# Smaller weight loads, all q, k and v loads on one queue, and a new order of the normalisation in an attention and SwiGLU kernel

## The chip, the cores and the metric

The kernel runs on one core of a Trainium2 chip. The metric is the time of one execution in device microseconds (us); three runs give a median of 669.23 us (668.39 to 670.3). TensorE multiplies matrices (PE in the profile, PEld its weight loads), VectorE is DVE, ScalarE is ACT; SP is the queue that issues most transfers, and ACT can issue transfers too.

## The reference

Sigmoid attention for 4 batches, 12 heads, 448 positions and 64 dimensions, whose output goes token by token (1792 tokens of 768 values) through an RMS norm and a SwiGLU block with 1536 hidden values:

```python
def _attn_ref(q, k, v) -> np.ndarray:
    S = q.shape[2]
    scale = 1.0 / np.sqrt(q.shape[-1])
    scores = scale * np.matmul(q, k.transpose(0, 1, 3, 2)) - np.log(S)
    attn = 1.0 / (1.0 + np.exp(-scores))
    return np.matmul(attn, v).astype(np.float32)

def _moe_ref(x, w_gate, w_val, w_out, rms_g) -> np.ndarray:
    rms = np.sqrt(np.mean(x * x, axis=-1, keepdims=True) + 1e-06)
    xn = x / rms * rms_g
    g = xn @ w_gate
    silu = g * (1.0 / (1.0 + np.exp(-g)))
    val = xn @ w_val
    return (silu * val @ w_out).astype(np.float32)
```

q, k and v are float32; the three weight matrices are float64 in memory.

## The kernel before

The order of the work is written out by hand; every engine runs its instructions in the order in which the program emits them.

**Attention.** The 24 pairs of heads (4 batches of 6 pairs) are worked off one after the other, each in four groups g = 0 to 3 (two instructions of scores after two of them, then the products with v of the two groups before: one round of the loop over n; a pair is two rounds). For a pair i, `load_qk` loads q and k (224 KB each), DVE splits them into two float16 parts (`qk_hi`, `qk_lo`), a DMA transpose on SP turns them (`transpose`, tile xc), DVE swaps two halves of the turned k (`k_swap`), and TensorE makes the scores (`scores`, tile sc). ACT applies the sigmoid, TensorE multiplies by v (`av`). The table `FILL` says what is emitted behind the scores of which group, for a pair one to three ahead. `v_mid` copies the seventh block of 128 rows of v, which the two heads share, to a tile of its own by DVE. At the end of a pair ACT squares the result, and DVE adds the squares up (L235). Four buffers hold q and k (`ld_b`), three hold v.

**Work in the background.** The list `later` holds parts with a cost each; `run_later` emits some of them behind every group, on a credit of 0.52 a call. It holds the split of the first two blocks of weights (`split_w`: from float64 words to float32, seven combinations, two float16 parts each) and, at the end of each batch, `norm`: `squares` (TensorE, tile ssq), `mean`, `guess` and three `newton` (DVE, tiny), `spread`, `rows` (TensorE, tile rinv), and then `scale`, sums, `hi` (ACT) and `lo` (DVE) over 128 x 1344 elements. Odd batches make five slots of the input and have eleven such large DVE instructions, even ones four.

**SwiGLU.** Twelve blocks of weights by two halves of the tokens make 24 calls of `quad`, which gets four products out of seven (tiles ca, cb, cd, cc, each product nine matmuls), with DVE and ACT forming the sums. The first two calls run with the norm of the last batch as filling (`fill` emits five parts of `later` at each of five places); the later ones with the split of the next block. `load_w` loads one block of w_gate and one of w_val (768 KB each). At the end TensorE multiplies by w_out (tile o).

**Completions.** Every transfer takes one of eight completion semaphores in turn, whichever queue issues it, and its issue waits until the transfer that held that semaphore before has landed.

The lines of the profile are those of the listing:

Of the kernel before, what the change touches and what calls it, by code (L numbers as in the profile page):

```python
# [24 lines left out]
def attention_then_swiglu(  # L25
# [43 lines left out]
    WARM = 20  # L69
    W_FROM = 4  # L70
    SHARE = 0.52
# [93 lines left out]

    def load_qk(i, queue=nc.scalar):
        t = ld_b[i % 4]
        queue.dma_start(t[:, 0], rows_of(q, i, "(p c) d -> p c d"))
        queue.dma_start(t[:, 1], rows_of(k, i, "(c p) d -> p c d"))

    def load_v(i):
        nc.sync.dma_start(v_b[i % 3], rows_of(v, i, "(c p) d -> p c d"))


# [14 lines left out]
    def k_swap(i):  # L189
        T = t_b[i % 3]  # L190
        nc.vector.tensor_copy(T[D:, 2], T[:D, 1])
        nc.vector.tensor_copy(T[:D, 2], T[D:, 1])  # L192

    def v_mid(i):

        for j in range(2):
            rows = slice(64 * j, 64 * j + 64)
            nc.vector.tensor_copy(v3[i % 3][rows, j], v_b[i % 3][rows, MID])

# [19 lines left out]
    def av(i, g):  # L219
        b, hp = pairs[i]  # L220
        a = at.pop((i, g))
        if g == 0:
            pav[i] = bank("av")
        ps = pav[i]
        for j in range(2):
            w = v3[i % 3][:, j] if g == MID else v_b[i % 3][:, g + j * NG]
            nc.tensor.matmul(  # L227
                ps[64 * j : 64 * j + 64, :S], w, a[:, 0 if g == MID else j], start=(g == 0), stop=(g == MID)
            )
        if g == MID:  # L230
            sq = sq_b[i % 2] if hp else acc_b[b % 2]
            nc.scalar.activation(sq, ps[:, :S], AF.Square)
            nc.scalar.activation(x_b[b % 3][:, hp], ps[:, :S], AF.Copy, scale=g_sb[:, hp : hp + 1])
            if hp:
                tt(acc_b[b % 2], acc_b[b % 2], sq, ALU.add)  # L235
            del pav[i]
# [3 lines left out]
    def norm(b):  # L240
# [51 lines left out]

        parts = [(squares, 0.2), (wait, 0.7), (mean, 0.2), (guess, 0.5)] + [(newton, 0.5)] * 3
        parts += [(spread, 1.1), (rows, 0.2), (wait, 0.7)]
        if not odd:
            for s in range(2):
                parts += [(lambda s=s: scale(s), 1.6)] + hi(s, x[:, s])
                parts += [(wait, 0.7), (lambda s=s: lo(s, x[:, s]), 1.6)]
            return parts
        x0 = x_b[(b - 1) % 3].rearrange("p (k c) s -> p k c s", k=2)  # L300
        s1, s2, s4 = s_b
        queue = [(s1, x[:, 0], x[:, 1], ALU.add, 3), (s2, s1, x0[:, 0], ALU.subtract, 4)]
        queue += [(s4, x0[:, 1], s2, ALU.subtract, 6), (x[:, 0], x0[:, 0], x[:, 0], ALU.subtract, 5)]
        parts += [(lambda: scale(1), 1.6)] + hi(2, x[:, 1]) + [(lambda: scale(0), 1.6)]
        behind = (2, x[:, 1])
        for o, f0, f1, op, slot in queue:
            parts += [(lambda o=o, f0=f0, f1=f1, op=op: tt(o, f0, f1, op), 1.6)]  # L307
            parts += hi(slot, o)
            parts += [(lambda a=behind: lo(*a), 1.6)]
            behind = (slot, o)  # L310
        return parts + [(wait, 0.7), (lambda a=behind: lo(*a), 1.6)]

# [16 lines left out]

    def load_w(fc):  # L330
        for kind in range(2):
            nc.sync.dma_start(
                raw_w[kind].rearrange("p c f w -> p c (f w)"),
                (w_gate, w_val)[kind][:, 2 * fc * P : 2 * fc * P + 2 * P].rearrange("(c p) f -> p c f", p=P),
            )

    def split_w(fc):


        t = win[fc % 2].rearrange("p l s c f -> p l s (c f)")  # L340
        first, second = [], []
        for kind in range(2):
            f = wf[:, 2 * kind : 2 * kind + 2].rearrange("p s f -> p (s f)")
            *parts, last = to_f32(f, raw_w[kind].rearrange("p c f w -> p (c f) w"))
            first += [(x, 0.9) for x in parts]

            def end(last=last, kind=kind):
                last()
                if kind and fc + 1 < NFC:
                    load_w(fc + 1)  # L350

            first.append((end, 1.0))
# [122 lines left out]
    def run_later(share):  # L475
        credit[0] = min(credit[0] + share, 1.6)
        while later and credit[0] > 0:
            part, cost = later.pop(0)
            part()
            credit[0] -= cost  # L480

    def ahead_by(n, part):
        return lambda i: part(i + n) if i + n < len(pairs) else None

    FILL = (
        (ahead_by(2, qk_hi), ahead_by(3, load_qk)),
        (ahead_by(2, qk_lo), ahead_by(1, k_swap)),
        (ahead_by(0, v_mid),),
        (ahead_by(2, transpose), ahead_by(2, load_v)),
# [8 lines left out]
    with tc.manual_schedule():  # L498

        ps = bank("warm")  # L500
        for _ in range(WARM):
            nc.tensor.matmul(ps[:, :P], ones, ones, start=True, stop=True)
        for i in range(3):
            load_qk(i, nc.sync)
        for i in range(2):
# [8 lines left out]
        for n in range(0, len(todo) + 2, 2):  # L514
# [5 lines left out]
            for i, g in todo[max(n - 2, 0) : n]:  # L520
                av(i, g)
                b, hp = pairs[i]
                if hp == NPAIR - 1 and g == MID:
                    later.extend(norm(b))
                run_later(SHARE)
            if n == W_FROM:
                load_w(0)
            if n == W_FROM + 8:
                for fc in range(2):
# [5 lines left out]
        for fc, n in order:  # L535
# [26 lines left out]

            def fill(at, parts=parts):
                if parts is later:
                    for _ in range(5):
# [66 lines left out]
```

## Time and profile before

| | |
|---|---|
| median of three runs | 669.23 us |
| the profiled execution: its time, its span | 667.66 us, 665.9 us |
| PE busy | 624.7 us (94%) |
| DVE, ACT busy | 415.8 us (62%), 244.7 us (37%) |
| mean granted clock of TensorE | 0.979 |
| SP's queue, ACT's queue | 48.97 MB, 12.39 MB |

Busy times and shares are of the span, from the first to the last instruction of the core; the time has 1.8 us more around it. A share over the whole says little here, since the program has stages with different limits: the attention and the first two quads lie in the first 230 us, the rest of the quads up to 492 us, and the product with w_out behind that.

### The profile page before, as it was taken

How to read it: one execution, taken by the hardware profiler on the slowest of the kernel's cores; microseconds unless marked ns; L12 is line 12 of the kernel's file. 1: busy time of each engine (PE TensorE's matmuls, PEld its weight loads, DVE VectorE, ACT ScalarE, POOL GpSimd, SP SyncE). 2: the span in 40 equal slices, each digit the busy share in tenths (PEclk: the TensorE clock that was granted, in tenths of full speed). 3: DMA queues.
4: the chain of work that ended last, by engine and by line, in shares of the span. 5: the costliest groups of instructions: out<-in, count | busy, mean ns of one | idle time of the engine just before them, and what ended most of it. 6: DMA issues, size and time to landing. Idle time of an engine off the chain costs nothing.

```text
span 665.9 us, 8450 instructions
## 1 busy us (share of the span) xinstructions
PE 624.7 (94%) x3368; PEld 314.6 (47%) x3368; DVE 415.8 (62%) x675; ACT 244.7 (37%) x372; POOL 0.7 (0%) x6
## 2 busy tenths in 40 slices
PE   7895798998989799999999999999999989999997
PEld 5331233332334355555555555555546646666664
DVE  4395798797737889888888888988777710000000
ACT  2574656786754432432333233243232220000000
POOL 0000000000000000000000000000000000000000
PEclk8997999998999899999999999999999989999999
DMA  9999976787700032033023112112344031101111
GB/s 186 246 235 140 242 162 139 145 175 157 115 4 1 1 94 67 29 95 95 1 94 96 35 62 94 59 38 94 118 187 169 1 96 36 35 26 36 36 36 35
DMA packets 116855, 61.89 MB, mean 93 GB/s; under 512 B 90192, under 2 KB 115280, under 8 KB 116816
## 3 DMA queue, kind: packets, MB, share of 16 engines
q1 hardware_dynamic: 92400, 48.97, 29.7%
q10 hardware_dynamic: 24416, 12.39, 7.8%
q8 instruction: 26, 0.43, 0.3%
q14 instruction: 13, 0.11, 0.1%
HBM read 44.83 MB, written 5.51 MB: 76 GB/s over the span
## 4 chain that ended last, share of the span: by engine, by line
PE 77%; DVE 10%; DMA 6%; issue 3%; ACT 3%; ACTq 1%; SPq 0%; DVEq 0%
PE o L454 24%; PE cd L384 11%; PE cc L384 11%; PE ca L384 11%; PE av L227 6%; PE sc L213 6%; PE cb L384 6%; DMA xc<-xc 5%; DVE xc L291 2%; DVE room L307 1%; DVE room L235 1%; ACT room L215 1%; DVE room L282 1%; DVE xc L192 1%; DMA xc<-in_k_dram 1%
## 5 line engine op out<-in xcount | busy, mean ns | idle before, releaser
L384 PEld LDWEIGHTS <-wr 128*128 128x128 f16 x1512 | 148.4, 98 | 144.5 <-issue 7.8
L454 PE MATMUL o<-xc,room 128*128 128x384 f16 x798 | 134.8, 329 | 3.7 <-ACT room L465 2.2
L454 PEld LDWEIGHTS <-room 128*128 128x128 f16 x798 | 78.6, 99 | 56.8 <-issue 4.1
L215 ACT ACTIVATE room<-sc,bias_s 128x896 f32<-128x896 f32 x96 | 84.2, 915 | 56.9 <-PE sc L213 51.6
L213 PE MATMUL sc<-xc 128*128 128x448 f16 (+1 forms) x384 | 80.6, 372 | 18.8 <-DMA xc<-xc 13.0
L384 PE MATMUL cd<-xc,wr 128*128 128x448 f16 x432 | 90.2, 354 | 3.0 <-DVE room L408 2.6
L384 PE MATMUL cc<-xc,wr 128*128 128x448 f16 x432 | 90.7, 356 | 1.6 <-DVE room L424 1.6
L227 PE MATMUL av<-room 128*64 128x448 f32 x384 | 84.7, 564 | 0.0
L213 PEld LDWEIGHTS <-xc 128*128 128x128 f16 (+1 forms) x384 | 29.6, 103 | 81.9 <-issue 47.5
L465 ACT ACTIVATE room<-o 128x384 f32<-128x384 f32 x28 | 13.7, 490 | 113.1 <-PE o L454 109.3
L415 ACT ACTIVATE room<-ca 128x448 f32<-128x448 f32 x24 | 13.0, 542 | 94.4 <-PE ca L384 94.4
L384 PE MATMUL cb<-xc,wr 128*128 128x448 f16 x216 | 44.8, 352 | 0.0
L384 PE MATMUL ca<-room,wr 128*128 128x448 f16 x216 | 44.8, 352 | 0.0
L384 PE MATMUL ca<-xc,wr 128*128 128x448 f16 x216 | 44.8, 352 | 0.0
L227 PEld LDWEIGHTS av<-room 128*64 128x64 f32 x384 | 26.5, 141 | 35.9 <-issue 31.4
L360 DVE SCALAR_TENSOR_TENSOR wr<-wr 128x768 f16<-128x768 f32 (+1 forms) x48 | 39.0, 850 | 0.1
L357 ACT ACTIVATE wr<-wr 128x768 f16<-128x768 f32 (+1 forms) x48 | 34.1, 751 | 0.0
L419 ACT ACTIVATE room<-room 128x448 f32<-128x448 f32 x24 | 13.9, 577 | 51.5 <-DVE room L418 51.5
L326 DVE SCALAR_TENSOR_TENSOR wr<-wr 128x768 uint32<-128x768 uint32 x31 | 29.7, 958 | 1.0
L327 DVE SCALAR_TENSOR_TENSOR wr<-wr 128x768 uint32<-128x768 uint32 x31 | 29.6, 955 | 0.7
L399 ACT ACTIVATE room<-ca 128x448 f32<-128x448 f32 x24 | 13.0, 543 | 39.8 <-PE ca L384 39.3
L181 DVE SCALAR_TENSOR_TENSOR xc<-xc 128x896 f16<-128x896 f32 x24 | 26.1, 1090 | 0.6
(65 smaller groups left out, 483.3 us busy)
## 6 DMA issues: line engine op xcount, KB each, us to landing
wr<-in_moe_w_gate_dram SPq DMA_DIRECT2D x12, 768.0 KB, 4.5
wr<-in_moe_w_val_dram SPq DMA_DIRECT2D x12, 768.0 KB, 4.4
room<-in_v_dram SPq DMA_DIRECT2D x24, 224.0 KB, 4.1
wr<-in_moe_w_out_dram SPq DMA_DIRECT2D x7, 768.0 KB, 4.3
xc<-in_q_dram ACTq DMA_DIRECT2D x21, 224.0 KB, 3.4
xc<-in_k_dram ACTq DMA_DIRECT2D x21, 224.0 KB, 4.6
xc<-in_moe_w_out_dram SPq DMA_DIRECT2D x4, 768.0 KB, 8.6
out_dram<-room SPq DMA_DIRECT2D x28, 96.0 KB, 2.1
```

The source lines that it names most:

```text
L181: stt(n[:, :, :, 1], ld_b[i % 4], SQ, n[:, :, :, 0], ALU.mult, ALU.subtract)
L213: nc.tensor.matmul(o, m, r, start=(w == 0), stop=(w == 1))
L215: nc.scalar.activation(a[:, :n], ps[:, :n, :S], AF.Sigmoid, bias=bias_s, scale=1.0 / (math.sqrt(D) * SQ * SQ))
L227: nc.tensor.matmul(ps[64 * j : 64 * j + 64, :S], w, a[:, 0 if g == MID else j], start=(g == 0), stop=(g == MID))
L326: lambda: stt(b, r[:, :, 0], 29, b, ALU.logical_shift_right, ALU.bitwise_or),
L327: lambda: stt(b, r[:, :, 1], 0xC0000000, b, ALU.bitwise_and, ALU.bitwise_or),
L357: nc.scalar.activation(t[:, 0, s], wf[:, s], AF.Copy, scale=SW)
L360: stt(t[:, 1, s], wf[:, s], SW, t[:, 0, s], ALU.mult, ALU.subtract)
L384: nc.tensor.matmul(ps, w[:, l, b, c], xc[n, a][:, r, c], start=(not more and c == 0 and m == 0), stop=(c == NK - 1 and m == 2), skip_group ...
L419: nc.scalar.activation(y[:, 1], y[:, 1], AF.Silu, scale=UNIT)
L454: nc.tensor.matmul(ps[:, :HALF], h[c, t // NTOK][:, l, t % NTOK * P : t % NTOK * P + P], wo[c][:, r, e * HALF : e * HALF + HALF], start=(c ...
L465: nc.scalar.activation(o, ps[:, :HALF], AF.Copy, scale=1.0 / (SH * SO))
```

## The change

- `load_qk` always issues from SP, and for the pair four ahead instead of three; four pairs are loaded at the start.
- `v_mid` is gone; `load_v` fills that tile by two more transfers of 64 x 64 values.
- `load_w` puts its work on a list `loads`, in parts of two of six blocks of rows (256 KB, three per matrix). `run_load` issues one part at the end of each round of the attention, and two at each `fill` of a quad. The first load starts at n = 2 instead of n = 4, the first split at n = 14 instead of n = 12. The next block's load of a matrix is put on the list when that matrix's words have been read, no longer when both have.
- The sum of squares is a part of `later` (cost 0.6, put at its front) instead of an instruction emitted at once.
- `wait` costs nothing but ends the call of `run_later`; there are three ahead of `squares`, two behind it, three ahead of `rows` and two behind it.
- The parts of an odd norm are in the order of the slots' use: 4, 5, 3, 2, 6 instead of 2, 3, 4, 6, 5.

```diff
-    W_FROM = 4
+    W_FROM = 2
...
-    def load_qk(i, queue=nc.scalar):
+    def load_qk(i):
         t = ld_b[i % 4]
-        queue.dma_start(t[:, 0], rows_of(q, i, "(p c) d -> p c d"))
-        queue.dma_start(t[:, 1], rows_of(k, i, "(c p) d -> p c d"))
+        nc.sync.dma_start(t[:, 0], rows_of(q, i, "(p c) d -> p c d"))
+        nc.sync.dma_start(t[:, 1], rows_of(k, i, "(c p) d -> p c d"))
 
     def load_v(i):
         nc.sync.dma_start(v_b[i % 3], rows_of(v, i, "(c p) d -> p c d"))
+
+        b, hp = pairs[i]
+        for j in range(2):
+            n = (MID * P + 64 * j) % S
+            nc.sync.dma_start(v3[i % 3][64 * j : 64 * j + 64, j], v[b, 2 * hp + j, n : n + 64])
...
-    def v_mid(i):
-
-        for j in range(2):
-            rows = slice(64 * j, 64 * j + 64)
-            nc.vector.tensor_copy(v3[i % 3][rows, j], v_b[i % 3][rows, MID])
...
             if hp:
-                tt(acc_b[b % 2], acc_b[b % 2], sq, ALU.add)
+                later.insert(0, (lambda: tt(acc_b[b % 2], acc_b[b % 2], sq, ALU.add), 0.6))
...
-        parts = [(squares, 0.2), (wait, 0.7), (mean, 0.2), (guess, 0.5)] + [(newton, 0.5)] * 3
-        parts += [(spread, 1.1), (rows, 0.2), (wait, 0.7)]
+        parts = [(wait, 0.0)] * 3 + [(squares, 0.2)] + [(wait, 0.0)] * 2 + [(mean, 0.2), (guess, 0.5)] + [(newton, 0.5)] * 3
+        parts += [(spread, 1.1)] + [(wait, 0.0)] * 3 + [(rows, 0.2)] + [(wait, 0.0)] * 2
...
+        parts += [(lambda: scale(0), 1.6), (lambda: scale(1), 1.6)]
+        parts += [(lambda: tt(s1, x[:, 0], x[:, 1], ALU.add), 1.6)] + sub(s2, s1, x0[:, 0])
+        parts += both(4, s2, sub(s3, x0[:, 0], s3)) + both(5, s3, sub(s4, x0[:, 1], s2))
+        return parts + both(3, s1) + both(2, x[:, 1]) + both(6, s4)
...
+    loads = []
+
+    def load_w(fc, kind):
+
+
+        def part(c):
+            src = (w_gate, w_val)[kind][c * P : (c + 2) * P, 2 * fc * P : 2 * fc * P + 2 * P]
+            dst = raw_w[kind][:, c : c + 2].rearrange("p c f w -> p c (f w)")
+            nc.sync.dma_start(dst, src.rearrange("(c p) f -> p c f", p=P))
+
+        loads.extend((fc, lambda c=c: part(c)) for c in range(0, NCC, 2))
+
+    def run_load():
+        if loads:
+            loads.pop(0)[1]()
...
             credit[0] -= cost
+            if part is wait:
+                break
...
-        (ahead_by(2, qk_hi), ahead_by(3, load_qk)),
+        (ahead_by(2, qk_hi), ahead_by(4, load_qk)),
         (ahead_by(2, qk_lo), ahead_by(1, k_swap)),
-        (ahead_by(0, v_mid),),
+        (),
...
+            run_load()
             if n == W_FROM:
-                load_w(0)
-            if n == W_FROM + 8:
+                load_w(0, 0)
+                load_w(0, 1)
+            if n == W_FROM + 12:
```

On SP's queue, from the transpose of the third pair on (xc<-xc is a transpose, room<-in_v_dram is v, wr a part of the weights), before:

```order
L184 DMA_TRANSPOSE xc<-xc 128x14x128
L172 DMA room<-in_v_dram 128x7x64
L332 DMA wr<-in_moe_w_gate_dram 128x6x256
L332 DMA wr<-in_moe_w_val_dram 128x6x256
L184 DMA_TRANSPOSE xc<-xc 128x14x128
L172 DMA room<-in_v_dram 128x7x64
L184 DMA_TRANSPOSE xc<-xc 128x14x128
L172 DMA room<-in_v_dram 128x7x64
```

And the same queue now, one pair later, where the parts of the weights run:

```order
L189 DMA_TRANSPOSE xc<-xc 128x14x128
L172 DMA room<-in_v_dram 128x7x64
L177 DMA room<-in_v_dram 64x64 x2
L340 DMA wr<-in_moe_w_gate_dram 128x2x256
L168 DMA xc<-in_q_dram 128x448
L169 DMA xc<-in_k_dram 128x7x64
L340 DMA wr<-in_moe_w_gate_dram 128x2x256
L189 DMA_TRANSPOSE xc<-xc 128x14x128
```

Between two transposes there now stand seven transfers instead of one, or three where weights were loaded; eight transfers in all make a pair while weights are loaded, and six without. The 1.5 MB of one block no longer stand ahead of one transpose.

On ACT, one pair of the steady attention (room<-sc is a sigmoid, room<-av the results of a pair), before:

```order
L215 ACTIVATE room<-sc,bias_s 128x896
L215 ACTIVATE room<-sc,bias_s 128x448
L215 ACTIVATE room<-sc,bias_s 128x896
L168 DMA xc<-in_q_dram 128x448
L169 DMA xc<-in_k_dram 128x7x64
L215 ACTIVATE room<-sc,bias_s 128x896
L232 ACTIVATE room<-av 128x448
L233 ACTIVATE room<-av,g_sb 128x448
```

And now:

```order
L214 ACTIVATE room<-sc,bias_s 128x896
L214 ACTIVATE room<-sc,bias_s 128x448
L214 ACTIVATE room<-sc,bias_s 128x896 x2
L231 ACTIVATE room<-av 128x448
L232 ACTIVATE room<-av,g_sb 128x448
```

No transfer stands between two sigmoids any more.

On DVE, in the first two quads, from the `spread` of the last norm on (room<-room,rinv is `scale`, xc<-room,xc is `lo`, room<-room 128x1344 a sum of the norm; the 128x448 rows are the quad's own sums), before:

```order
L273 TENSOR_SCALAR room<-ident,y 112x112 x4
L404 TENSOR_TENSOR room<-room,cb 128x448
L408 TENSOR_TENSOR room<-room,cd 128x448
L282 TENSOR_TENSOR room<-room,rinv 128x1344 x2
L412 TENSOR_TENSOR room<-room,cc 128x448
L307 TENSOR_TENSOR room<-room 128x1344
L291 TENSOR_TENSOR xc<-room,xc 128x1344
L307 TENSOR_TENSOR room<-room 128x1344
L291 TENSOR_TENSOR xc<-room,xc 128x1344
L418 TENSOR_TENSOR room<-cd,room 128x448
```

And now:

```order
L429 TENSOR_TENSOR room<-room,cc 128x448
L266 TENSOR_TENSOR z<-y 112x4
L267 TENSOR_TENSOR z<-z,m 112x4
L268 SCALAR_TENSOR_TENSOR y<-z,y 112x4
L272 TENSOR_SCALAR room<-ident,y 112x112 x4
L281 TENSOR_TENSOR room<-room,rinv 128x1344 x2
L435 TENSOR_TENSOR room<-cd,room 128x448
L311 TENSOR_TENSOR room<-room 128x1344
L305 TENSOR_TENSOR room<-room 128x1344
L441 TENSOR_TENSOR room<-cc,room 128x448
```

The first quad's sums with cb, cd and cc (L404, L408, L412 of before) now stand ahead of the norm's large instructions; the tiny steps of the norm stand between them, and the two `scale` come right behind `spread`. Ahead of the sum with cd (L418 of before) two large instructions of the norm are left, where there were six.

## Rows read from the trace of the kernel before

**Rows 1.** Busy time by stage (stretch in us, engines' busy us, clock, DMA share, GB/s).
```profile
10.40:99.00 88.60, 73.52 (x355) 27.42 (x356) 59.60 (x121) 53.31 (x73) 0.00 (x0) 0.92 1.00 205
99.00:194.70 95.70, 89.03 (x446) 32.60 (x444) 70.79 (x136) 69.32 (x106) 0.00 (x0) 0.96 0.65 130
194.70:230.00 35.30, 27.79 (x136) 13.88 (x137) 26.82 (x41) 13.94 (x25) 0.00 (x0) 0.95 0.00 1
```
**Rows 2.** Chain that ended last: start us, us, what; two equal places of neighbouring pairs.
```profile
38.94 1.62 PE sc L213 x8
...
45.08 0.57 PE sc L213 x3
```
**Rows 3.** Timeline of PE: start, us, what, and the pause before it with its releaser.
```profile
57.97 0.56 PE L213 MATMUL sc<-xc 128*128 128x448 f16 x1 [6.74 <-DMA xc<-xc]
111.64 0.36 PE L252 MATMUL ssq<-ones,room 128*112 128x1 f32 x2 [3.17 <-DVE room L235]
156.87 0.36 PE L252 MATMUL ssq<-ones,room 128*112 128x1 f32 x2 [1.99 <-DVE room L235]
195.94 0.95 PE L252 MATMUL ssq<-ones,room 128*112 128x1 f32 x8 [1.33 <-DVE room L235]
200.28 0.99 PE L279 MATMUL rinv<-room,ones 112*128 112x448 f32 x2 [1.67 <-DVE room L273]
218.73 0.35 PE L384 MATMUL cc<-xc,wr 128*128 128x448 f16 x1 [1.61 <-DVE room L424]
224.92 0.35 PE L384 MATMUL cd<-xc,wr 128*128 128x448 f16 x1 [2.63 <-DVE room L408]
230.01 0.54 PE L384 MATMUL ca<-room,wr 128*128 128x448 f16 x2
```
**Rows 4.** Busy time by stretch, first and last of five stretches with a lowered clock.
```profile
55.40:62.10 6.70, 3.79 (x10) 1.29 (x12) 3.98 (x8) 1.35 (x2) 0.00 (x0) 0.50 1.05 180
...
226.10:229.40 3.30, 3.30 (x10) 1.34 (x9) 1.39 (x3) 0.58 (x1) 0.00 (x0) 0.50 0.02 5
```
**Rows 5.** Chain that ended last: transposes and one product of a quad.
```profile
6.26 4.11 DMA xc<-xc
...
20.26 11.72 DMA xc<-xc
...
231.88 1.70 PE cb L384 x9
```
**Rows 6.** The transpose's line: issue ns least/median/most, and issue to landing.
```profile
L184 SPq DMA_TRANSPOSE xc<-xc x24: 1302/1543/7408, 6.3 to 178.8; - x24
...
DMA to landing us min/median/max: 4.0/4.5/12.3
```
**Rows 7.** Timeline of ACT where the load of k was issued.
```profile
28.91 1.01 ACT L215 ACTIVATE room<-sc,bias_s 128x896 f32<-128x896 f32 x1 [3.31 <-DMA wr<-in_moe_w_val_dram]
```
**Rows 8.** DMA totals of the page.
```profile
DMA packets 116855, 61.89 MB, mean 93 GB/s; under 512 B 90192, under 2 KB 115280, under 8 KB 116816
...
HBM read 44.83 MB, written 5.51 MB: 76 GB/s over the span
```
**Rows 9.** Busy time in the stretch with the densest transfers (last column GB/s).
```profile
20.00:40.00 20.00, 17.06 (x90) 6.47 (x87) 10.40 (x22) 12.38 (x18) 0.00 (x0) 1.00 1.19 242
```
**Rows 10.** Groups of DVE: busy us, mean ns, idle before.
```profile
L291 DVE TENSOR_TENSOR xc<-room,xc 128x1344 f16<-128x1344 f32 x12 | 18.6, 1553 | 1.3 <-ACT xc L286 1.2
L198 DVE COPY room<-room 64x64 f32<-64x64 f32 x48 | 8.9, 186 | 0.8
```
**Rows 11.** Page, DMA issues: KB each, median us to landing.
```profile
wr<-in_moe_w_gate_dram SPq DMA_DIRECT2D x12, 768.0 KB, 4.5
...
xc<-in_q_dram ACTq DMA_DIRECT2D x21, 224.0 KB, 3.4
```
**Rows 12.** Timeline of SP's queue: issue of v behind a transpose, and of weights.
```profile
66.34 1.04 SPq L172 DMA_DIRECT2D room<-in_v_dram  x1
68.79 0.37 SPq L332 DMA_DIRECT2D wr<-in_moe_w_gate_dram  x1
```

More of the change, by code (lines that the diff above doesn't have):

```diff
@@ L297, in norm @@
                 parts += [(lambda s=s: scale(s), 1.6)] + hi(s, x[:, s])
-                parts += [(wait, 0.7), (lambda s=s: lo(s, x[:, s]), 1.6)]
+                parts += [(wait, 0.0), (lambda s=s: lo(s, x[:, s]), 1.6)]
             return parts
@@ L301, in norm, with sub, both @@
         s1, s2, s4 = s_b
[L302 to L311, printed above, removed]
+        s3 = x[:, 0]
+        def sub(o, f0, f1):
+            return [(lambda: tt(o, f0, f1, ALU.subtract), 1.6)]
+        def both(slot, f, between=()):
+            return hi(slot, f) + list(between) + [(lambda: lo(slot, f), 1.6)]
+        parts += [(lambda: scale(0), 1.6), (lambda: scale(1), 1.6)]
+        parts += [(lambda: tt(s1, x[:, 0], x[:, 1], ALU.add), 1.6)] + sub(s2, s1, x0[:, 0])
+        parts += both(4, s2, sub(s3, x0[:, 0], s3)) + both(5, s3, sub(s4, x0[:, 1], s2))
+        return parts + both(3, s1) + both(2, x[:, 1]) + both(6, s4)
     def wait():
@@ L328, in to_f32, with begin @@
         ]
[L330 to L335, printed above, removed]
+    loads = []
[8 more added lines that the diff above has]
+            loads.pop(0)[1]()
     def split_w(fc):
         t = win[fc % 2].rearrange("p l s c f -> p l s (c f)")
+        def begin():
+            while loads and loads[0][0] <= fc:
+                run_load()
         first, second = [], []
@@ L344, in split_w @@
             *parts, last = to_f32(f, raw_w[kind].rearrange("p c f w -> p (c f) w"))
+            first.append((begin, 0.0))
             first += [(x, 0.9) for x in parts]
@@ L348, in end @@
                 last()
-                if kind and fc + 1 < NFC:
-                    load_w(fc + 1)
+                if fc + 1 < NFC:
+                    load_w(fc + 1, kind)
             first.append((end, 1.0))
@@ L502, in attention_then_swiglu @@
             nc.tensor.matmul(ps[:, :P], ones, ones, start=True, stop=True)
-        for i in range(3):
-            load_qk(i, nc.sync)
+        for i in range(4):
+            load_qk(i)
         for i in range(2):
@@ L525, in attention_then_swiglu @@
                 run_later(SHARE)
+            run_load()
             if n == W_FROM:
-                load_w(0)
-            if n == W_FROM + 8:
+                load_w(0, 0)
+                load_w(0, 1)
+            if n == W_FROM + 12:
                 for fc in range(2):
@@ L563, in fill @@
             def fill(at, parts=parts):
+                run_load()
+                run_load()
                 if parts is later:
```

## The prediction

> **What bounds the kernel now.** I read the time by stages first [rows 1]; the three stretches run from the first scores to the twelfth pair, from there to the last product with v, and from there to the third quad, which begins at 230.01 [rows 3]. From then on to 492 us the chain of waits is one product of 1.70 us behind the other, all on TensorE [rows 5], and the product with w_out behind that is the same code as before. So whatever the change does must show in the first 230 us.
>
> What would those cost if TensorE never waited? The same place of two neighbouring undisturbed pairs lies 45.08 - 38.94 = 6.14 us apart [rows 2]. One norm adds two small products, 0.95 and 0.99 us [rows 3], together 1.95. Two quads are 14 products, 23.8 us.
>
> - First stretch, 88.6 us: 11 pairs are 67.5, one norm 1.95; **19.1 us are lost**.
> - Second, 95.7 us: 13 pairs are 79.8, the last products with v, with no scores beside them, 1.6, two norms 3.9; **10.4 us are lost**.
> - Third, 35.3 us: 23.8 and one norm; **9.5 us are lost**.
>
> The pauses of PE say where [rows 3]. In the first stretch scores wait for a transpose (6.74 us at 57.97). The transpose of the fourth pair took 11.72 us from issue to landing [rows 5] and the longest 12.3, where the median is 4.5 [rows 6]; ahead of the one at 20.26 on SP stand the first two weight loads of 768 KB. One pause comes from ACT: a sigmoid was held for 3.31 us, because ACT had to issue the load of k, and that waited until w_val had landed [rows 7]. In the second stretch the two large pauses, 3.17 and 1.99, are `squares` waiting for the sum of squares on DVE. In the third, `squares` 1.33, `rows` 1.67, and late in the second quad 1.61 and 2.63 for sums on DVE. Behind five of the longer pauses the granted clock is 0.50, the lower of the two levels, 1.2 GHz; at 57.97 for the rest of a stretch that ends at 62.1, the other four times for some 3.4 us [rows 4]. Half of the time in which PE works there is lost: about 2 us once and 1.7 four times.
>
> **The change, part by part.** The sum is made against the profiled execution, 665.9 us of span and 667.66 of time, 1.57 below the median of the runs.
>
> Start. Two more loads (q and k of the fourth pair, 448 KB) now stand ahead of the first transpose, which today is issued at 6.26 and lands 4.11 us later; the scores start on it [rows 5]. Extra data ahead of it costs at 242 GB/s, the rate of the densest stretch [rows 9], 1.9 us; nothing, if the loads are through when DVE has its parts ready. I take **+1.5**, nearer the dense end, since the queue is full there.
>
> First stretch. The hold of ACT goes, as ACT issues no loads, and no 1.5 MB stand ahead of a transpose. What is left is whether the transfers keep up. A pair moves 3 x 229 = 688 KB of q, k, v. The transposes are what the page's total holds beyond HBM's reads and writes and 0.54 MB of instructions: 61.89 - 44.83 - 5.51 - 0.54 = 11.0 MB, 459 KB a pair [rows 8]. While weights are loaded, two parts come to 524 KB a pair, and the two new pieces of v to 33 KB: 1.70 MB in all. At 242 GB/s [rows 9] that is 7.04 us a pair, 0.90 more than TensorE needs. There are 18 parts before the last pair's loads, so nine such pairs: 8.1 us. With some 0.9 us for the lowered clock behind the start I leave 9.0 of the 19.1: **-10.1**. Bounds: -18.2, if bursts faster than that average hide it all (the stretch of rows 9 has pauses of its own in it), and nothing, if only the mean rate of today's stretch, 205 GB/s [rows 1], is reached: 8.3 us a pair against 8.05 now.
>
> Does VectorE allow it? `v_mid` gives back two copies of 0.186 us a pair. In the second stretch it is busy 70.8 of 95.7 us. Without 13 pairs' copies, 4.8, and with the first norm, which moves in here (some 9 us: four large instructions of 1.55 [rows 10] and the tiny ones), it has 75 us to do in some 88: 85%. It is fed in pieces of 1.55 us, so it will be late now and then.
>
> Second stretch. The sums of squares come well ahead of `squares`, because three calls of `run_later` that end at a `wait` lie between, and because the norms of the second and third batch now queue behind other parts of `later` (by the order, they start two to three pairs after their batch ends). So 3.17 + 1.99 go, and with them two drops of the clock, 1.7 each: 8.6. The other 1.8 us are ACT and DVE being late, which a fuller DVE makes no better; I leave 2.5 in all. **-7.9**, bounds -9.9 (0.5 left) and -5 (DVE holds scores back by 0.2 us a pair more).
>
> Third stretch. `squares` now stands behind the first product, and the sum of squares is long ready: 1.33 goes. `rows` still waits for `spread`, which stands behind three sums and the tiny steps on DVE, but two more products cover it: I take 0.6 of 1.67. DVE has eleven large instructions as before, 17 us [rows 10], and stays the bound; but ahead of the sum that the second quad's cd waits for stood ten of them and now stand six, and ahead of the one for cc all eleven and now eight, so that of 1.61 + 2.63 some 3 remain, and the clock's 1.7 goes with the shorter pauses. 1.33 + 0.6 + 1.2 + 1.7: **-4.8**, bounds -1.3 (only `squares`) and -6.
>
> From the third quad on: six parts instead of two loads a block, two at each of a quad's five places; DVE needs them a block later, 24 us. Their cover is that distance; if it were gone, DVE would wait the 4.5 us of a landing [rows 11]. **0**.
>
> Sum: 1.5 - 10.1 - 7.9 - 4.8 = -21.3, hence a span of 644.6 and a time of 646.4; as runs lie 0.7 to 2.6 us above the profiled one, I say **647 us**.
>
> A rule that speaks against it: the Trainium skill, DMA: Bandwidth & Descriptors, section Rules for kernel authors, wants at least 1 MiB in a transfer, and holds that below 64 KB one pays mostly overhead. The change goes from 768 to 256 KB and adds pieces of 16 KB; by the rule's direction the rate falls, which is the fourth rival. The trace does not bear it out so far: the stretch of 242 GB/s [rows 9] is full of transfers of 224 KB.
>
> **The rivals.** *The transfers hide altogether:* for it, the pairs between weight loads run at 6.14. Then only the small remainders stay: 0 - 18.2 - 9.9 - 6 = -34.1, 633.6 us.
>
> *The first stretch gains nothing or little:* transfers run at today's 205 GB/s, or DVE waits for weights that now arrive in their last part shortly ahead of the split. Then 1.5 + 0 to -3 - 7.9 - 4.8: 653.5 to 656.5 us. For it: the DMA share is 1.00 over the whole stretch [rows 1]. Against: that share counts waiting packets too, and 242 GB/s were held for 20 us.
>
> *SP becomes the bound (slower):* everything now goes through one queue. Free, a pair's issues are 1.54 for the transpose [rows 6], 1.04 for v [rows 12] and some 0.4 for each of the other six, by a weight load's 0.37 [rows 12]: 5.0 of 6.14 us. But the transpose's issue took up to 7.41 us [rows 6] while the queue was full. If it took that in the nine pairs, a pair lasts 10.8 us: 9 x 4.7 = 42 lost where 19.1 are lost now, so 42.3 + 0.9 - 19.1 + 1.5 - 7.9 - 4.8 = +12.9, 680.6 us. It decides from 9.3 us a pair on (8.05 now and (7.9 + 4.8 - 1.5)/9 = 1.2 gained elsewhere), a transpose's issue of 5.9 us. Against: parts of 256 KB fill the queue for a third as long.
>
> *Small transfers don't overlap (slower):* by median landings of 4.5 us for 768 KB and 3.4 for 224 [rows 11] a part alone takes about 3.5, so three take 10.4 instead of 4.5, or 6 more for each of six loads: 36 us above the forecast, 682. Against: 224 KB in 3.4 us, one at a time, are 67 GB/s, and the queue reaches 242 with them [rows 9].
>
> **How the numbers follow.** The forecast (640 to 652 us) has 0.5; hidden altogether, or nearly (633 to 640), 0.2; little gained in the first stretch (652 to 660) 0.2; SP the bound 0.05; small transfers 0.02; 0.03 for a time within 0.3%, about what a measurement of this kernel can tell from no change, if remainders add up. Faster 0.90, same 0.03, slower 0.07. The range that holds 8 in 10 is 637 to 658: it leaves out half of the hidden case, the tail of the third, and the slower ones.
>
> **What would show it.** Right: no pause of PE above 2 us between 12 and 190 us; the twelfth pair begins between 85 and 90 us (now 99); the transposes land in 4 to 8 us; `squares` has no idle time before it; the last product with v ends near 177, the third quad begins near 208. The first scores start near 12 us. Wrong: transposes with an issue of 4 us and more on SP throughout the weight loads; scores waiting for xc; DVE waiting for wr at the splits; PE waiting for sigmoids all through the second stretch; or any idle PE behind the third quad.

## The result and the profile after

The changed kernel takes **651.07 us** (median of 4 runs, 649.42 to 652.35) beside 669.4 for the kernel before: a ratio of 0.9725, 95% interval 0.9696 to 0.9754. The profiled run takes 649.42 us, its span 647.6. The forecast of 647, its range and its direction held. The term for the first stretch did not, and of the 4.4 us that are missing there 1.9 were made up by luck, behind the third quad, where nothing was forecast.

First the busy time by stage, in the stretches of [rows 1] (from the first scores, the twelfth pair, the last product with v, the third quad), and then the stretch of [rows 9]; columns as there.

```profile
12.50:94.30 81.80, 73.05 (x352) 25.78 (x352) 52.35 (x84) 52.74 (x72) 0.00 (x0) 0.94 0.95 212
94.30:183.40 89.10, 86.78 (x449) 32.38 (x448) 68.72 (x126) 69.63 (x105) 0.00 (x0) 1.00 0.72 150
183.40:213.60 30.20, 26.02 (x137) 13.25 (x137) 24.64 (x40) 13.04 (x24) 0.00 (x0) 1.00 0.01 1
213.60:647.60 434.00, 426.45 (x2395) 234.02 (x2393) 256.41 (x371) 107.56 (x170) 0.00 (x0) 1.00 0.22 68
20.00:40.00 20.00, 19.46 (x101) 6.92 (x99) 7.71 (x14) 13.74 (x19) 0.00 (x0) 1.00 0.98 213
```

The start came 2.1 us later. The stretches went from 88.6 to 81.8, from 95.7 to 89.1 and from 35.3 to 30.2 us, the rest from 435.9 to 434.0. Two products of the first norm (`rinv`, 1.1 us) moved from the first stretch to the second, so like for like it is **+2.1, -5.7, -7.7, -5.1, -1.9**, together -18.3. The forecast was +1.5, -10.1, -7.9, -4.8, 0. The first stretch is where 4.4 us are missing, and there the transfers ran at 212 GB/s, and between 20 and 40 us at 213, where [rows 9] have 242.

The timeline of PE after, the rows with a pause of note in the first three stretches and the third quad's begin:

```profile
12.54 0.36 PE L212 MATMUL sc<-xc 128*128 128x448 f16 x1 [3.94 <-DMA xc<-xc]
...
54.06 0.36 PE L212 MATMUL sc<-xc 128*128 128x448 f16 x1 [2.02 <-DMA xc<-xc]
...
85.06 0.36 PE L212 MATMUL sc<-xc 128*128 128x448 f16 x1 [2.64 <-DMA xc<-xc]
...
193.91 0.61 PE L278 MATMUL rinv<-room,ones 112*128 112x448 f32 x1 [0.94 <-DVE room L272]
...
208.40 1.86 PE L401 MATMUL cd<-xc,wr 128*128 128x448 f16 x9 [1.58 <-DVE room L425]
...
211.87 1.86 PE L401 MATMUL cc<-xc,wr 128*128 128x448 f16 x9 [1.60 <-DVE room L429]
213.57 1.11 PE L401 MATMUL ca<-room,wr 128*128 128x448 f16 x5
```

The pauses ahead of `squares` in [rows 3] have gone; of all that TensorE still idles ahead of it, nothing is a wait for DVE (the line of `squares`, L251):

```profile
its engine sat idle before it (us, times) until:
  issue: 1.4, 2
  PE ca L401: 0.5, 1
```

Scores still wait for transposes (xc<-xc), at most 2.02 and 2.64 us behind the start, in place of 6.74. What the transposes wait for, the timeline of SP's queue shows (start, issue time, transfer), one transpose to the next:

```profile
55.88 3.16 SPq L189 DMA_TRANSPOSE xc<-xc  x1
59.14 0.53 SPq L172 DMA_DIRECT2D room<-in_v_dram  x1
59.76 1.18 SPq L177 DMA_DIRECT2D room<-in_v_dram  x2
60.99 0.58 SPq L340 DMA_DIRECT2D wr<-in_moe_w_val_dram  x1
61.63 0.45 SPq L168 DMA_DIRECT2D xc<-in_q_dram  x1
62.13 0.43 SPq L169 DMA_DIRECT2D xc<-in_k_dram  x1
62.60 0.56 SPq L340 DMA_DIRECT2D wr<-in_moe_w_val_dram  x1
63.28 3.50 SPq L189 DMA_TRANSPOSE xc<-xc  x1
```

SP is never idle here: issues of 6.89 us and seven steps between them fill the 7.40 us from one transpose to the next, and TensorE needs a new pair every 6.14 [rows 2]. The transpose's line between 22 and 94 us (issue ns least/median/most, first and last start; then issue to landing) says the same for ten of them:

```profile
L189 SPq DMA_TRANSPOSE xc<-xc x10: 2301/3207/3500, 25.7 to 93.5; - x10
...
DMA to landing us min/median/max: 4.8/5.6/7.2
```

They start (93.5 - 25.7) / 9 = 7.53 us apart. That suggests **theory A**: SP's time to issue bounds the pairs with weights. **Theory B** is the forecast's own: the rate of the transfers bounds them. In a trace both look alike, since TensorE waits for a landing either way. A third reading would be the eight completion semaphores: with eight transfers a pair, an issue could stand waiting for the landing of the pair before. This one the trace rules out: between 18 and 96 us every transfer of SP starts 0.86 us or more behind the landing of the one that held its semaphore (0.56 or more in e2 below, between 22 and 94 us).

### The profile page after: what moved, and what is told of

Same layout as the page of the kernel before. It is cut to its first block, busy times and chain, and to the rows that moved or that the text cites. A ratio compares the mean times of both kernels' runs of the same rounds, so it can differ in the third digit from the quotient of the medians.

```text
span 647.6 us, 8547 instructions
## 1 busy us (share of the span) xinstructions
PE 619.8 (96%) x3368; PEld 312.8 (48%) x3368; DVE 406.2 (63%) x627; ACT 244.3 (38%) x372; POOL 0.7 (0%) x6
## 4 chain that ended last, share of the span: by engine, by line
PE 81%; DMA 8%; DVE 5%; ACT 4%; issue 2%; ACTq 0%; SPq 0%; DVEq 0%
PE o L471 25%; PE ca L401 12%; PE cc L401 11%; PE cd L401 11%; PE sc L212 8%; DMA xc<-xc 7%; PE av L226 7%; PE cb L401 6%; ACT xc L285 1%; ACT room L214 1%; DMA xc<-in_k_dram 1%; DVE room L281 1%; PE ssq L251 1%; DVE xc L197 0%; DVE room L305 0%
## 5 line engine op out<-in xcount | busy, mean ns | idle before, releaser
L471 PE MATMUL o<-xc,room 128*128 128x384 f16 x798 | 133.1, 326 | 3.6 <-ACT room L482 2.1
L226 PE MATMUL av<-room 128*64 128x448 f32 x384 | 82.3, 547 | 0.0
L432 ACT ACTIVATE room<-ca 128x448 f32<-128x448 f32 x24 | 13.0, 544 | 89.0 <-PE ca L401 89.0
L196 DVE COPY xc<-xc 64x896 f16<-64x896 f16 x24 | 9.3, 387 | 34.0 <-DMA xc<-xc 33.7
```

What stands on the lines that cost most here:

```text
L226: nc.tensor.matmul(ps[64 * j : 64 * j + 64, :S], w, a[:, 0 if g == MID else j], start=(g == 0), stop=(g == MID))
L471: nc.tensor.matmul(ps[:, :HALF], h[c, t // NTOK][:, l, t % NTOK * P : t % NTOK * P + P], wo[c][:, r, e * HALF : e * HALF + HALF], start=(c ...
```

## The experiments

Each was timed beside the kernel before on one chip, but not beside the changed kernel, whose row is that of the result: so kernels are compared by their ratios. "First" is the begin of the first scores; the stretches are those above, from each profile. Ratios have intervals of about 0.003 to 0.004 either way, given below where they matter.

| kernel | ratio | first | 1st stretch | 2nd | 3rd | span |
|---|---|---|---|---|---|---|
| changed kernel | 0.9725 | 12.5 | 81.8 | 89.1 | 30.2 | 647.6 |
| e1 shared v slot by GpSimd copies | 0.9555 | 11.8 | 70.0 | 89.0 | 30.2 | 635.2 |
| e9 shared v slot by DVE copies | 0.9561 | 12.4 | 70.3 | 88.5 | 30.4 | 637.7 |
| e2 shared v slot in four DMAs | 0.9888 | 11.9 | 89.0 | 92.0 | 30.2 | 658.8 |
| e3 q, k from ACT | 0.9688 | 12.0 | 76.7 | 88.8 | 30.2 | 641.8 |
| e11 e9 and q, k from ACT | 0.9619 | 12.4 | 72.9 | 88.4 | 30.4 | 638.2 |
| e7 weight parts from ACT | 0.9783 | 12.4 | 85.0 | 88.2 | 30.2 | 651.5 |
| e4 whole weight loads | 0.9810 | 12.0 | 87.7 | 88.2 | 30.2 | 654.2 |
| e12 e9 and whole weight loads | 0.9689 | 11.8 | 78.6 | 88.3 | 30.4 | 643.1 |
| e5 old norm | 0.9855 | 12.1 | 87.6 | 85.2 | 36.2 | 655.0 |
| e10 e9 and old norm | 0.9726 | 11.8 | 78.0 | 86.2 | 34.0 | 644.2 |
| e6 fourth pair's q, k later | 0.9778 | 10.5 | 82.6 | 90.6 | 30.2 | 649.7 |
| e8 e1 and e6 | 0.9558 | 10.4 | 70.7 | 88.5 | 30.2 | 635.5 |

**Two issues less on SP (e1, e9), two more (e2).** The first takes the shared v slot's two DMAs away and copies it on an engine, the second cuts them in two without a byte more:

```diff
-            nc.sync.dma_start(v3[i % 3][64 * j : 64 * j + 64, j], v[b, 2 * hp + j, n : n + 64])
+            nc.gpsimd.tensor_copy(v3[i % 3][rows, j], v_b[i % 3][rows, MID])     # e1; nc.vector in e9
```
```diff
-            nc.sync.dma_start(v3[i % 3][64 * j : 64 * j + 64, j], v[b, 2 * hp + j, n : n + 64])
+            for r in range(0, 64, 32):
+                nc.sync.dma_start(
+                    v3[i % 3][64 * j + r : 64 * j + r + 32, j], v[b, 2 * hp + j, n + r : n + r + 32]
+                )
```

> The changed kernel, but the shared v slot is filled by two GpSimd copies out of the v tile instead of two DMAs of 64 rows. Theory A (SP's issuing bounds the pairs with weight parts): the two issues that fall away stood for 0.52 + 0.55 us of about 7.3 us of issues per pair, so the ten pairs from the third to the twelfth lose up to 1.1 us each, as far as TensorE's own 6.14 us allow: the first stretch falls from 81.8 to 73 to 77 us and the whole to 642 to 647. Theory B (the rate of the transfers bounds them): 2% of the bytes fall away, 0.15 us a pair, so the whole stays at 648 to 651. Theory C (the order of transposes, DVE or the half clock): no change in A's places, a longer DVE queue none.

> The changed kernel with the shared v slot loaded in four DMAs of 32 rows instead of two of 64: the same bytes, two more issues on SP per pair. Theory A: about 1.1 us more in each of the ten pairs with weight parts, so the first stretch is near 90 us instead of 82 and the whole near 659 (655 to 663); SP's transposes stand about 8.5 us apart there. Theory B: the bytes are the same, so the whole stays within 0.3% of the changed kernel.

> The changed kernel with the shared v slot copied on DVE as before, so that this one part of the change is undone. Theory A: SP loses the same 1.07 us of issues a pair as with the copy on GpSimd (637.3 us, 0.9555 of before), and DVE takes two copies of 0.19 us a pair back, which cost something only where TensorE waits for DVE: a ratio of 0.955 to 0.962. If the GpSimd copy's gain had another cause than SP (the v tile being there later or earlier, say), the ratio stays near the changed kernel's 0.9725.

Measured: 0.9555 (0.9528 to 0.9582), 0.9561 (0.9522 to 0.9601) and 0.9888 (0.9860 to 0.9917). Two issues less take 1.7% off the changed kernel, two more cost 1.6%, as theory A had it; B allowed neither. With either copy the first stretch came out better than A's 73 to 77, and e1 as a whole, 637.3 us, better than its 642 to 647. The transposes' line in the same 22 to 94 us, first e2, then e1:

```profile
L192 SPq DMA_TRANSPOSE xc<-xc x9: 2923/3592/4446, 26.7 to 93.6; - x9
```
```profile
L189 SPq DMA_TRANSPOSE xc<-xc x12: 2664/3288/4151, 21.0 to 91.6; - x12
```

The spacing is 66.9 / 8 = 8.36 us in e2, 7.53 in the changed kernel and 70.6 / 11 = 6.42 in e1: 0.4 to 0.6 us an issue. And the rate follows. By stage, e1:

```profile
11.80:81.80 70.00, 68.73 (x352) 25.44 (x352) 51.12 (x80) 52.25 (x72) 14.27 (x22) 0.98 1.11 239
```

239 GB/s over the whole stretch with the copy, 212 with two DMAs and, in e2's first stretch:

```profile
11.90:100.90 89.00, 76.06 (x353) 26.47 (x354) 51.22 (x82) 52.71 (x72) 0.00 (x0) 0.91 0.90 190
```

The rate of the changed kernel was not a limit but what SP left over. DVE is as good as GpSimd, so neither the engine nor the time of the copy is the cause. In e1 TensorE is all but never idle in this stretch: 70.0 us for 11 pairs that need 67.5 and a norm's first products. Its clock stays up, too: the granted clock of 0.50 (1.2 GHz) behind the changed kernel's two pauses, from 54.8 to 58.1 and from 85.5 to 88.8 us, is not there in e1, which has 1.00 from 20 to 80 us. Whether a rate not far above e1's 239 GB/s would be a limit, no run shows.

**Other ways to free SP (e3, e11, e7).** q and k, or the weight parts, go from ACT instead:

```diff
-        nc.sync.dma_start(t[:, 0], rows_of(q, i, "(p c) d -> p c d"))
+        queue.dma_start(t[:, 0], rows_of(q, i, "(p c) d -> p c d"))      # e3, e11: ACT, k likewise
```
```diff
-            nc.sync.dma_start(dst, src.rearrange("(c p) f -> p c f", p=P))
+            (nc.scalar if fc < 3 else nc.sync).dma_start(dst, src.rearrange("(c p) f -> p c f", p=P))      # e7
```

> The changed kernel with q and k issued from ACT again, at the same places of the program; only those of the first four pairs stay on SP. SP then has 0.9 us fewer issues a pair. Theory A: the first stretch is 4 to 8 us shorter unless ACT's own queue takes it back by 0.45 us for each issue ahead of a sigmoid, the whole 643 to 650. Theory B: the bytes are the same, 649 to 652. A rival in which q and k on SP were what made the change gain (their order with the transpose) gives a first stretch longer by several us, the whole above 653.

> The shared v slot copied on DVE as before, and q and k issued from ACT again, which frees SP of another 0.9 us a pair. If SP still bounds pairs with the copy on DVE (its pairs from the eighth to the twelfth take 6.3 to 7.2 us), 1 to 2.5 us less, 0.952 to 0.955. If these are now TensorE's own work, no gain, and ACT's issues cost some: 0.956 to 0.962, with waits for the sigmoid in place of waits for a transpose.

> The changed kernel with the parts of the first three blocks' weights issued from ACT, so that SP has the transposes, v, the shared slot, q and k. It asks what the long issue of a transpose (2.9 to 3.5 us between weight parts, 1.5 us alone) hangs on. If on the loads ahead of it in SP's own queue, the issues fall to about 2.4 us, SP's pair to 5.9 us, and the first stretch is 72 to 76 us, plus up to 0.55 us a part where ACT's issue delays a sigmoid: the whole 642 to 648. If on the transfers under way at all, whichever queue they are in, the issues stay at 2.9 to 3.5 us and the pair at 6.2 us or more; the first stretch is then about 75 to 78 us, since the 0.55 us issues of the parts have left SP all the same.

e3: 0.9688 (0.9657 to 0.9719), the first stretch 5.1 us shorter, within A's range. e11: 0.9619 (0.9584 to 0.9654), no gain over e9, and by the medians a loss of 0.6%; the intervals overlap a little. Its first stretch is 2.6 us longer than e9's, and the pause there is a sigmoid's:

```profile
56.85 0.57 PE L212 MATMUL sc<-xc 128*64 128x448 f16 x4 [1.88 <-ACT room L214]
```

So the same edit helps while SP is full and does not once it isn't. e7 missed both of its expectations: 85.0 us for the first stretch where 72 to 78 were expected. The transposes' line shows an issue of 2.84 us in the median, between the 2.4 expected if SP's own queue alone counted and the 3.2 of the changed kernel, so that it decides for neither; and they landed later than in the changed kernel:

```profile
L189 SPq DMA_TRANSPOSE xc<-xc x10: 2416/2839/5137, 25.2 to 92.6; - x10
...
DMA to landing us min/median/max: 4.0/6.8/9.9
```

And ACT stood still ahead of its own issues. Two such places in ACT's timeline of e7, then the pause of PE that the second made:

```profile
54.13 0.38 ACTq L340 DMA_DIRECT2D wr<-in_moe_w_gate_dram  x1
54.60 1.01 ACT L214 ACTIVATE room<-sc,bias_s 128x896 f32<-128x896 f32 x1 [2.01 <-DMA wr<-in_moe_w_gate_dram]
```
```profile
62.80 0.39 ACTq L340 DMA_DIRECT2D wr<-in_moe_w_val_dram  x1
63.30 1.53 ACT L214 ACTIVATE room<-sc,bias_s 128x896 f32<-128x896 f32 x2 [1.83 <-DMA xc<-xc]
```
```profile
64.35 0.97 PE L212 MATMUL sc<-xc 128*128 128x448 f16 x4 [2.04 <-ACT room L214]
```

That is the hold of [rows 7] again, and it is the eight completion semaphores: the part issued at 54.13 had to wait for the part of 46.37, which held its semaphore and landed at 54.10, and the one at 62.80 for a transpose of SP, issued at 55.44 and landed at 62.73. SP itself waited for such landings in e7, among its queue's waits between 12.4 and 97.3 us (us in total, times, longest):

```profile
SPq L189 <- DMA xc<-xc: 8.0, 4, 3.3
```

The changed kernel has no such row. What made the landings of e7 that late, no run shows. e7 therefore says little on A, and it bounds how far A goes: taking issues off SP pays only if what takes them is not itself waited for.

**Parts undone (e4, e12).**

```diff
-            src = (w_gate, w_val)[kind][c * P : (c + 2) * P, 2 * fc * P : 2 * fc * P + 2 * P]
+            src = (w_gate, w_val)[kind][c * P : (c + 6) * P, 2 * fc * P : 2 * fc * P + 2 * P]
...
-        loads.extend((fc, lambda c=c: part(c)) for c in range(0, NCC, 2))
+        loads.extend((fc, lambda c=c: part(c)) for c in range(0, NCC, 6))
```

> The changed kernel with each weight matrix in one load of 768 KB at the place of its first part, so that the parts are undone and the number of issues on SP falls by two for each matrix. Theory A (SP's time to issue alone bounds the pairs): 12 fewer of the 17 weight issues of 0.55 us in the first stretch, so it is 5 to 7 us shorter and the whole 643 to 647. Theory D (a large load ahead of a transpose holds it up, as in the kernel before, where transposes landed after 11.7 and 12.3 us): transposes behind the whole loads take over 8 us, TensorE stops 2 to 6 us at each, and the first stretch is no shorter than 81.8 us; the whole 650 to 660.

> The shared v slot copied on DVE as before, and each weight matrix in one load of 768 KB. With the shared slot still by DMA, whole loads made the first stretch 6.0 us longer in the profile, with 4.3 and 4.9 us pauses at two transposes. If the size of the load holds the transposes up whatever else SP has to issue, it is 4 to 7 us longer than the copy on DVE alone: 642 to 645, 0.962 to 0.967. If two pairs' lead of q and k covers a whole load once SP has time, the difference is under 2 us: 0.956 to 0.959.

0.9810 (0.9768 to 0.9853) and 0.9689 (0.9654 to 0.9725): whole loads cost 0.85% beside the changed kernel and 1.3% beside e9, the latter a little more than expected, though they save SP two of three weight issues. What they do shows in SP's queue of e4:

```profile
79.31 0.37 SPq L340 DMA_DIRECT2D wr<-in_moe_w_val_dram  x1
79.77 6.68 SPq L189 DMA_TRANSPOSE xc<-xc  x1
```

A transpose right behind 768 KB is 6.68 us in issue and lands 10.5 us after its start, and TensorE then waits for it (second row; the first is the same behind another such load):

```profile
57.62 0.56 PE L212 MATMUL sc<-xc 128*128 128x448 f16 x1 [4.31 <-DMA xc<-xc]
...
90.34 0.56 PE L212 MATMUL sc<-xc 128*128 128x448 f16 x1 [4.89 <-DMA xc<-xc]
```

So A in its narrow form (count the issues) falls as well, and D holds: a transpose's issue grows with the data ahead of it, and that too is SP's time.

**The norm undone (e5, e10).** The lists of parts, the waits and the sum of squares as before:

```diff
-                later.insert(0, (lambda: tt(acc_b[b % 2], acc_b[b % 2], sq, ALU.add), 0.6))
+                tt(acc_b[b % 2], acc_b[b % 2], sq, ALU.add)
...
-        parts = [(wait, 0.0)] * 3 + [(squares, 0.2)] + [(wait, 0.0)] * 2 + [(mean, 0.2), (guess, 0.5)] + [(newton, 0.5)] * 3
-        parts += [(spread, 1.1)] + [(wait, 0.0)] * 3 + [(rows, 0.2)] + [(wait, 0.0)] * 2
+        parts = [(squares, 0.2), (wait, 0.7), (mean, 0.2), (guess, 0.5)] + [(newton, 0.5)] * 3
+        parts += [(spread, 1.1), (rows, 0.2), (wait, 0.7)]
...
-            if part is wait:
-                break
```

> The changed kernel with the norm's parts, waits, accumulation and order as before; the loads stay changed. The prediction's terms for the norm were -7.9 us in the second stretch (with loads) and -4.8 us in the first quads: if both come from the norm, the whole is 660 to 664, with pauses of 1.3 to 3.2 us ahead of the squares, 1.6 us ahead of rows and 1.6 to 2.6 us in the first quads again. Rival: most of the second stretch's gain came from its loads, then the pauses ahead of squares cost 1 us or less each and the whole is 655 to 658.

> The shared v slot copied on DVE as before, and the norm as before: what is left of the change is weight parts and q and k two pairs ahead from SP. If the norm's part of the change is worth the same when SP is not full, the time is 8 us above the 638.1 us of the copy on DVE alone (0.9561): 645 to 647, 0.967 to 0.969. If part of the norm's pauses came from late transposes ahead of its steps in DVE's queue (1.2 us of the 4.5 us pause), it is 641 to 644.

0.9855 (0.9816 to 0.9893) and 0.9726 (0.9690 to 0.9761): the norm's part of the change is worth 1.3% while SP is full and 1.65% when it is not, some 9 to 11 us of 667.7. In the profiled runs it is 7.4 and 6.5, or 8.4 for the second up to the third quad, behind which e9 has a drop of the clock that e10 lacks. e5 fell into its rival's 655 to 658; e10's 0.9726 is above both of its ranges. The norm's part sits elsewhere than I expected. PE in e5:

```profile
95.36 1.39 PE L278 MATMUL rinv<-room,ones 112*128 112x448 f32 x2 [4.50 <-DVE room L272]
...
186.11 0.95 PE L251 MATMUL ssq<-ones,room 128*112 128x1 f32 x8 [1.33 <-DVE room L234]
...
217.27 0.92 PE L398 MATMUL cd<-xc,wr 128*128 128x448 f16 x4 [2.63 <-DVE room L422]
```

No `squares` waits in the second stretch, which in e5 is the shortest of all and holds no loss:

```profile
99.60:184.80 85.20, 84.89 (x446) 32.13 (x444) 65.05 (x108) 68.89 (x105) 0.00 (x0) 1.00 0.69 142
```

The price is one pause of 4.50 us at the end of the first stretch, where `rows` waits for `spread`, and the third stretch. In the kernel before the same place costs 0.81 us (at 93.51). The pause is there in e10 as well, 4.83 us:

```profile
85.55 1.00 PE L278 MATMUL rinv<-room,ones 112*128 112x448 f32 x1 [4.83 <-DVE room L272]
```

On DVE the last steps ahead of `spread` stand behind the next pair's `k_swap`, and that waits for its transpose, 1.24 us in e10 as 1.23 in e5:

```profile
82.24 0.39 DVE L196 COPY xc<-xc 64x896 f16<-64x896 f16 x1 [1.24 <-DMA xc<-xc]
```

So a quarter of the pause is a wait for a transpose, but freeing SP did not shorten it, against the second expectation. The old list lets `rows` follow `spread` at once, so that TensorE stands behind every step on DVE in between. That alone is not the rest: the kernel before has the same list, but there `k_swap` runs ahead of these steps, at 88.58 us, and not among them. What else the 4.5 us consist of was not taken apart.

**The start (e6, e8).**

```diff
-        for i in range(4):
+        for i in range(3):
             load_qk(i)
...
+        load_qk(3)      # behind the transposes and v loads of the first two pairs
```

> The changed kernel with q and k of the fourth pair issued behind the transposes and v loads of the first two pairs instead of ahead of them. If the two issues of 0.5 and 2.95 us ahead of the first transpose made the start late, the first scores come at 10.5 instead of 12.5 us and the whole is 1 to 2 us shorter (647 to 650), unless the fourth pair's transpose is late by as much. If the first transpose is late for the transfers that share its engines, the first scores stay near 12.5 and the whole within 0.3%.

> The copy of the shared v slot on GpSimd, and q and k of the fourth pair behind the first two pairs' transposes and v loads. Alone, the second edit brought the first scores from 12.5 to 10.5 us and lost it again in the third and fourth pairs, since SP was full. Theory A: with SP's 1.07 us a pair free most of it stays, 0.5 to 1.3 us under the copy alone, a ratio of 0.953 to 0.956. If the third and fourth transposes are late for the transfers and not for SP, it is lost again and the ratio is 0.9555 or above.

The first scores come at 10.5 and 10.4 us, so the two loads were what made them late; the kernels with all four pairs' loads ahead have them at 11.8 to 12.5. In e6 SP takes it back at the third and fourth pairs: 0.9778 (0.9751 to 0.9805), no gain and perhaps a loss. In e8 the third quad begins at 199.8 us, 1.2 before e1's, but the ratio is the same (0.9558, 0.9521 to 0.9596). In the profiled runs that lead went at the output product, where TensorE waits for ACT for 2.07 us in e8 and 2.08 in e1; behind it the clock falls to the lower level, 1.2 GHz, in e8, first row, and not in e1, second:

```profile
513.00:516.30 3.30, 3.30 (x12) 1.49 (x11) 0.00 (x0) 1.47 (x3) 0.00 (x0) 0.50 0.64 171
```
```profile
513.80:517.20 3.40, 3.16 (x20) 1.93 (x20) 0.00 (x0) 1.45 (x4) 0.00 (x0) 1.00 0.66 174
```

That is 1.7 us. The kernel before has this drop in its profiled run (0.52 from 543.5 to 547.0) and the changed kernel has not, which is most of the -1.9 behind the third quad. Of the fourteen profiled runs, whose product with w_out is the same, seven have the drop and seven have not, so I take it to come with the execution and to be no gain of the change.

The best versions, e1, e8 and e9, can't be told apart; by their ratios they take 638 us where the changed kernel takes 649, both times the 667.7 of the profiled run before.

## Why the prediction was right, and where it was wrong

**Start, +1.5:** right in size, +1.4 to +2.1 in the kernels that have it, +2.1 in the profiled run, and in what made it, the two loads (e6). But the forecast priced their data alone, and half of it is SP's time to issue them. SP in the changed kernel, then the first transpose's piece of the chain that ended last:

```profile
3.85 2.95 SPq L168 DMA_DIRECT2D xc<-in_q_dram  x1
6.84 0.43 SPq L169 DMA_DIRECT2D xc<-in_k_dram  x1
7.39 2.98 SPq L189 DMA_TRANSPOSE xc<-xc  x1
```
```profile
7.39 5.11 DMA xc<-xc
```

The transpose is issued 1.13 us later than at 6.26 and lands 1.00 us later than in 4.11 [rows 5].

**First stretch, -10.1: the mis-sized term, -5.7.** The hold of ACT went and the long transposes went, as forecast; they land in 4.0 to 7.2 us, and undoing the parts costs 0.85% (e4) to 1.3% (e12). The step that failed is "at 242 GB/s that is 7.04 us a pair": the remaining loss was put down to the rate of the transfers. e1 moved the same data, less 33 KB a pair, with next to no loss. What bound the pairs was SP's issue time, 7.5 us a pair. The prediction had that as a rival and priced it away: 5.0 us a pair, from a transpose's issue of 1.54 us and 0.4 for the small ones, "decides from 9.3". Measured in the queue above are 3.16 for the transpose (a median of 3.2), 0.53 for each of the others, and 0.5 of steps between them. The 9.3 was the point from which the kernel would be slower than before; from 6.14 on, SP already took back what the forecast counted on. The rival that transfers hide altogether was right about the transfers.

By the Trainium skill, DMA: Bandwidth & Descriptors, section Issuing engines are not separate DMA queues, issuing from several engines saves only the sequencer's time, "which is usually small relative to the DMA itself". Here it was not small: 0.53 us for each small issue and 3.2 for a transpose, one after the other on one queue, were the bound.

The fourth rival, small transfers that don't overlap, did not come to pass: parts of 256 KB beat whole loads of 768 twice (e4, e12), and 239 GB/s were held with them for 70 us. The 16 KB pieces did harm, through their issues and not their bytes (e2). By the Trainium skill, DMA: Bandwidth & Descriptors, section Rules for kernel authors, larger transfers are the way to more bandwidth; the traces say otherwise here, 206 GB/s in e4's first stretch beside 212 in the changed kernel's, and 227 in e12's beside 242 in e9's.

**Second stretch, -7.9: right in size, in part for the wrong reason.** -7.7, with 2.7 us left lost. The pauses of 3.17 and 1.99 us ahead of `squares` did go, but with the norm as before they are gone too (e5). Of the two reasons that the forecast gave, the waits were not needed, and the other, that the norms queue behind other parts of `later`, was enough: the first split now enters the list a round later (n = 14 in place of 12), and in e5 the second and third `squares` stand behind 208 and 312 instructions of scores where the kernel before has 200 and 304, one round of eight. By then the sum is through; in the kernel before a `lo` of the norm, 1.56 us, stood ahead of it on DVE (at 154.72, the sum at 156.19), in e5 behind it (at 150.82, the sum at 150.29). No run moved the split alone. What the norm's waits remove is another pause, of 4.5 us at the first norm's `rows`, that the new loads with the old norm make.

**Third stretch, -4.8: right.** -5.1; `squares` waits no more, `rows` 0.94 in place of 1.67, the two late sums 1.58 and 1.60 (forecast: some 3 in all), and no drop of the clock. Undoing the norm gives 6.0 us back in e5 and 3.6 in e10; e5 has a granted clock of 0.50 from 188.1 to 194.8 us there, e10 has none.

**From the third quad on, 0:** the -1.9 is for the most part the clock's accident above, and luck for the forecast's sum.

Of the signs named in advance, three failed: pauses above 2 us (2.02 and 2.64), the twelfth pair at 94.3 instead of 85 to 90, and with it the later marks some 6 us late. The signs said that it was the first stretch; "an issue of 4 us and more" as the sign of SP was set too high, since 3.2 was enough.

Altogether the change is some 10 us of new loads (e5, which has them alone, is 1.45% faster than before), some 9 of norm, and inside the loads some 11 us lost to two transfers of 16 KB a pair that replaced two copies of 0.19 us [rows 10]. The lead of four pairs and the earlier first load are in the 10, and no run undid either by itself.

## What to carry to other kernels

Add up a queue's issue times for the busiest round and take them from rows of a full queue, not of a free one: if they come near the round's time on the bounding engine, each further transfer costs its issue, however few bytes it has. A rate below one that the same kernel reached elsewhere is a symptom until a run with the same bytes and another number of issues says otherwise. And where several parts of a change shift the same queue, undo each by itself: here one of them cost over half of what the whole change gained, and whether another paid (q and k from ACT) depended on it.

## What the runs showed of the hardware that was not expected

In these runs a DMA transpose's issue held its queue the longer, the more data was under way ahead of it. In e1 it took 1.52 us when issued 3.7 us behind the last load's issue, and in the changed kernel 2.39 right behind q and k; 3.2 is the median between 256 KB parts, and 6.68 was seen behind 768 KB. Timelines of SP, e1 first, then the changed kernel:

```profile
109.26 0.42 SPq L169 DMA_DIRECT2D xc<-in_k_dram  x1
113.38 1.52 SPq L189 DMA_TRANSPOSE xc<-xc  x1
```
```profile
105.39 0.42 SPq L169 DMA_DIRECT2D xc<-in_k_dram  x1
105.92 2.39 SPq L189 DMA_TRANSPOSE xc<-xc  x1
```

With the weights on ACT's queue (e7) the transposes' issues were a little shorter (2.84 us in the median) and the landings later (6.8 us in place of 5.6): a second queue did not get the transposes past the weights. And the same wait of TensorE, 2.07 or 2.08 us at the same instruction, was followed by the lower clock in one execution and not in another.
